# Softmax attention mixed with a Mish layer on one core: a run-time bound on the scores with a second attention behind a branch, a Mish with one reciprocal for four elements, and a later spread of its first layer

## The chip, the cores and the metric

The kernel runs on one core of a Trainium2 chip. A core has five engines that work beside each other, each through its own list of instructions in order: TensorE (PE, matrix products, with its weight loads shown apart as PEld), VectorE (DVE), ScalarE (ACT, functions such as exp), GpSimd (POOL) and SyncE (SP, which issues DMAs). They wait for each other through semaphores. The metric is device time in microseconds (us); the kernel before took 981.92 us in the median of 3 runs (981.38 to 982.19).

## What is computed

```python
S, D, F, H = 2048, 640, 1536, 32          # Dh = 20, bf16 in and out
q, k, v = split(x @ wqkv)                 # x: 2048 x 640
a = softmax(q @ k.T / sqrt(20)) @ v       # 32 heads
a = a @ wo
h = x @ w1 + b1                           # 2048 x 1536
b = (h * tanh(log(1 + exp(h)))) @ w2      # Mish between two layers
g = sigmoid(sum(x * gate_w))              # one value a row
out = g * a + (1 - g) * b
```

The inputs are normal numbers times 0.05 (the Mish layer's weights smaller still).

## The kernel before

**Attention.** Scores are computed transposed: a tile holds 128 keys by 512 queries. One such tile of one head is a unit. The units are ordered in 32 groups of 64: a group is one set of four heads (`p`, 8 of them) and one chunk of 512 queries (`qc`, 4 of them), and runs over 16 blocks of keys (`j`) and the four heads (`t`). A head has only 20 dimensions, so four heads lie on four 32-row strips of PE. The exponentials are taken without subtracting the row maximum. One iteration of the main loop takes 3 units, the next 2, and so on (`WIDTHS`), which makes 819 iterations; a group is 25 or 26 of them. Group 1 begins with iteration 25, group 25 with 640, group 28 with 716, group 30 with 768, group 31 with 793.

In iteration i the list of instructions gets, in this order: the score matmuls of iteration i+1 (`emit_qk`, L616), the exponential of iteration i on ACT from PSUM to a bf16 tile `E` (`emit_exp`, L626), the products of earlier exponentials with V into the accumulator `acc` (`emit_pv`, L656), the steps that are due (`run_later`), and then other PE work (`pump`). V has a column of ones, so that `acc` also gets the sum of each row; at the end of a group `normalise` (L632 to L646) transposes `acc` on DVE, divides, and keeps the result in one of 50 spare tiles, `cells`.

**The other PE work** is cut into chains with a start, a due iteration and a list of pieces, each with a nominal cost in ns: projections to Q and K (`kq_chain`, L255) and V (`v_chain`, L276), the first Mish layer (`h_chain`, L342, 48 tiles of 128 x 512), the second one (`b_chain`, L372, 32 chains of 12 pieces), the output projection (`wo_chain`, L412). `pump` goes through them in order of due iteration. It emits pieces while the work done is behind the summed share that is wanted, up to `BURST` = 700 ns of nominal cost in an iteration, and without that limit when a chain marked hard is about to be late. It also keeps PE at a floor of 0.54 of the iteration's nominal time, with pieces ahead of their share and, where there are none, with matmuls on a tile of ones that nobody reads (`busy_matmul`, L570). Chains accumulate in two PSUM banks (`pp`), which DVE empties.

**Mish** of one tile takes exp(h) on ACT (L305) and then works on DVE on n = e(e+2) and h n/(n+2): two operations at once (L308, L311), a reciprocal in four quarters, one an iteration (L317), and two operations at the end (L320, L324). The result stays in a `cells` tile until all `b_chain`s of its chunk of rows are done. At most two tiles are in the making. The `h_chain`s of the four chunks follow each other from iteration 35 on, 146.6 iterations each, the last one up to iteration 621; the `b_chain`s of a chunk follow 146.6 iterations behind.

**The end.** After the last exponential come the last products with V, `normalise`, eight matmuls (L760), four operations on DVE (L768) that put together the last 512 rows, and four stores (L776), two issued by SP and two by ACT. L804 is the end of the program: waits for all landings, drains, and a barrier over all engines.

Of the kernel before, what the change touches and what calls it, by code (L numbers as in the profile page):

```python
# [14 lines left out]
PSUM = bass.MemoryType.PSUM  # L15


class Chain:
# [11 lines left out]
    def share(self, i):  # L30
        if i >= self.due:
            return self.cost
        if i <= self.start:
            return 0.0
        return self.cost * (i - self.start) / (self.due - self.start)


@with_exitstack
def kernel(
# [25 lines left out]
    inv_sqrt_dh = float(DH) ** -0.5  # L65
    WIDTHS = (3, 2)
    N_CAP = 1.0e30
    NCELL = 50
# [16 lines left out]
    tp = ctx.enter_context(tc.tile_pool(name="tp", bufs=2))  # L85
# [17 lines left out]
    busy = consts.tile([P, QC], BF16, tag="busy")  # L103
    acc = accpool.tile([P, QC], F32, tag="acc")
# [72 lines left out]
    ]  # L177
    iters = []
# [11 lines left out]
    def it_at(G, j=0):  # L190
        k = G * 64 + 4 * j
        return it_of[k] if k < len(units) else NI
# [18 lines left out]
    now = [0]  # L211

# [17 lines left out]
    def transpose_chain(c, u, start, due):  # L230
        def piece():
            ps = pp.tile([P, KT * P], BF16, tag="pp", name="ps")
            transpose_tile(c, u, ps, nc.vector)
            x_ready[c] += 1
# [11 lines left out]
    def kq_chain(wpad, chunk, get_dst, start, due, before=None, copy=None):  # L246
# [16 lines left out]
        def finish():  # L263
            (copy or nc.vector.tensor_copy)(out=get_dst(), in_=box["ps"][:, :])  # L264
# [3 lines left out]
    def v_chain(sts, w, c0, n, h0, start, due, gate=False):  # L268
# [16 lines left out]
        def finish():  # L285
            nh = n // DH
            for i, st in enumerate(sts):
                nc.vector.tensor_copy(
# [13 lines left out]
    def mish_steps(ft, c, h):  # L302
        e = mp.tile([P, QC], F32, tag="e", name="e")
        r = mp.tile([P, QC], F32, tag="r", name="r")
        nc.scalar.activation(e[:, :], h[:, :], ACT.Exp)  # L305

        def first_ops():
            nc.vector.scalar_tensor_tensor(  # L308
                out=e, in0=e, scalar=2.0, in1=e, op0=ALU.add, op1=ALU.mult
            )  # L310
            nc.vector.tensor_scalar(  # L311
                out=r, in0=e, scalar1=N_CAP, scalar2=2.0, op0=ALU.min, op1=ALU.add
            )

        def rec(k):
            a, b = k * P, (k + 1) * P
            nc.vector.reciprocal(out=r[:, a:b], in_=r[:, a:b])  # L317

        def last_ops():
            nc.vector.scalar_tensor_tensor(  # L320
                out=r, in0=e, scalar=N_CAP, in1=r, op0=ALU.min, op1=ALU.mult
            )
            t = taken.pop((ft, c))
            nc.vector.tensor_tensor(out=t, in0=h, in1=r, op=ALU.mult)  # L324
# [3 lines left out]
        at(now[0] + 1, first_ops)  # L328
        for k in range(4):
            at(now[0] + 2 + k, (lambda k=k: rec(k)))  # L330
        at(now[0] + 6, last_ops)

    def h_chain(ft, c, start, due):
# [16 lines left out]
        def finish():  # L350
            h = mp.tile([P, QC], F32, tag="h", name="h")
            nc.vector.tensor_scalar(  # L352
# [11 lines left out]
    def b_chain(s, half, start, due):  # L364
# [15 lines left out]
        def finish():  # L380
            if c not in Bt:
                Bt[c] = stage.tile([P, NU, D], BF16, tag="stage", name="Bt")
            nc.vector.tensor_scalar(  # L383
# [7 lines left out]
            if b_done[c] == 2 * NU:  # L391
                cells.extend(act[(ft, c)] for ft in range(FT))
# [9 lines left out]
    def wo_chain(s, half, start, due, ps_list, base=None, dst=None):  # L402
# [17 lines left out]
        def finish():  # L420
# [5 lines left out]
            else:  # L426
                o = dst()[:, cols]
            nc.vector.scalar_tensor_tensor(  # L428
# [21 lines left out]
    def pads(p):  # L450
# [9 lines left out]
        return fn  # L460

# [45 lines left out]
    span = (m1 - m0) / (NQC + 1)  # L507
    for c in range(NQC):
# [3 lines left out]
        for k, (x, y) in enumerate(spread(a + span + 8, a + 2 * span + 8, 2 * NU)):  # L512
# [8 lines left out]
    for k, (x, y) in enumerate(spread(it_at(G7[last_qc]) + 6, NI - 2, 2 * NU)):  # L521
# [8 lines left out]
        chains.append(wo_chain(s, k % 2, x, y, list(range(NQ - 1)), dst=get_R))  # L530
    chains.sort(key=lambda ch: (ch.due, ch.start))
# [91 lines left out]
    def emit_exp(i):  # L623
# [3 lines left out]
            E[:, 0 : n * QC], S_of.pop(i)[:, 0 : n * QC], ACT.Exp, scale=inv_sqrt_dh  # L627
# [4 lines left out]
    def normalise(G, p, qc):  # L632
        T1 = tp.tile([P, NS, 32], F32, tag="T1", name="T1")
# [15 lines left out]
    pv_hold = [-1]  # L649

    def emit_pv(limit):
        while pv_next[0] + 4 <= limit and pv_hold[0] < now[0]:
# [156 lines left out]
```

## Time and profile before

The profiled execution took 983.07 us; its span, from the first instruction's start to the last one's end, is 981.0 us. The 2.07 us between them lie outside the program. The profiled execution is 1.15 us over the median of the runs.

| part of the span | us |
|---|---|
| up to the first exponential of the attention | 0 to 11.2 |
| the exponentials of the 819 iterations on ACT | 11.2 to 971.1 |
| last products, normalise, last rows, issue of the stores | 971.1 to 978.4 |
| landing of the last stores, waits, drains, barrier | 978.4 to 981.0 |

| engine | busy us | share of the span |
|---|---|---|
| ACT | 959.3 | 98% |
| PE | 841.8 | 86% |
| DVE | 493.2 | 50% |
| POOL | 19.9 | 2% |

A busy time is the union of an engine's instructions. Matmuls are pipelined, so PE's busy share says little about its room. Records of neighbouring instructions on one engine can overlap; then the mean of one is longer than what one more would cost. A row of a group reads: line, engine, operation, written<-read, shapes, count, then busy us and mean ns of one, then the engine's idle time before them and what ended it.

### The profile page before, as it was taken

The numbers are of one execution on the slowest core, as the hardware profiler recorded it, in microseconds if no ns is written. First come the engines' busy times: TensorE is split into PE (matmuls) and PEld (weight loads), VectorE is DVE, ScalarE is ACT, GpSimd is POOL, SyncE is SP. The second block draws the span as 40 slices with busy tenths as digits, with TensorE's granted clock in tenths as the row PEclk, the third lists the DMA queues.
The fourth block names the chain that finished last, engine by engine and source line by source line (L and its number), as shares of the span: only waits on it lengthen the run. The fifth ranks groups of instructions, "written<-read, shape, count | busy, mean of one in ns | idle before, by whom it ended". The sixth has DMA issues, their size and how long they took to land.

```text
span 981.0 us, 14426 instructions
## 1 busy us (share of the span) xinstructions
PE 841.8 (86%) x5834; PEld 309.9 (32%) x5914; DVE 493.2 (50%) x785; ACT 959.3 (98%) x873; POOL 19.9 (2%) x33
## 2 busy tenths in 40 slices
PE   8888888888888888888888888888888888888896
PEld 4333322223333332333222232322323333333332
DVE  4337565566567556655665655565554112112223
ACT  6999999999999999999999999999999999999995
POOL 5000000000000000000000000000000000000000
PEclk9999999999999999999999999999999999999998
DMA  9000010000100010000102001000000000000000
GB/s 272 16 1 21 1 29 1 22 20 2 29 1 21 1 29 1 21 21 1 29 1 54 1 21 29 1 21 1 1 1 1 1 1 14 8 14 15 14 15 34
DMA packets 23515, 19.28 MB, mean 20 GB/s; under 512 B 10025, under 2 KB 22201, under 8 KB 23449
## 3 DMA queue, kind: packets, MB, share of 16 engines
q1 hardware_dynamic: 20696, 11.66, 4.6%
q0 software_dynamic: 1520, 5.94, 2.0%
q8 instruction: 46, 0.75, 0.3%
q10 hardware_dynamic: 1232, 0.76, 0.3%
q14 instruction: 21, 0.16, 0.1%
HBM read 15.73 MB, written 2.62 MB: 19 GB/s over the span
## 4 chain that ended last, share of the span: by engine, by line
ACT 56%; issue 32%; PE 11%; DVE 1%; ACTq 0%
ACT E L626 54%; PE Sp L616 4%; ACT e L305 2%; PE acc L656 2%; PE ps L255 1%; PE ps L412 1%; PE ps L570 1%; PE ps L276 1%; PE acc L679 0%; PE ps L220 0%; DVE ot L768 0%; PE ps L342 0%; DVE xT L228 0%; PE ps L683 0%; PE sa L220 0%
## 5 line engine op out<-in xcount | busy, mean ns | idle before, releaser
L626 ACT ACTIVATE E<-Sp 128x1536 bf16<-128x1536 f32 (+1 forms) x819 | 938.5, 1278 | 4.5 <-PE acc L656 2.5
L616 PE MATMUL Sp<-qT,kT 32*128 32x512 bf16 x2048 | 320.7, 381 | 122.2 <-ACT E L626 103.7
L616 PEld LDWEIGHTS <-kT 32*128 32x128 bf16 x2048 | 128.0, 91 | 345.0 <-issue 310.1
L656 PE MATMUL acc<-E,VA 128*21 128x512 bf16 x2048 | 203.4, 386 | 0.2
L317 DVE RECIPROCAL r<-r 128x128 f32<-128x128 f32 x192 | 166.6, 915 | 1.3
L570 PE MATMUL ps<-busy 128*128 128x512 bf16 (+1 forms) x273 | 88.9, 383 | 1.7 <-DVE ot L428 0.3
L656 PEld LDWEIGHTS <-VA 128*21 128x21 bf16 x2048 | 50.4, 89 | 116.5 <-issue 116.5
L352 DVE TENSOR_SCALAR h<-ps,b1f 128x512 f32<-128x512 f32 x48 | 35.8, 746 | 93.5 <-PE ps L342 88.3
L372 PE MATMUL ps<-w_sb,cell 128*128 128x320 bf16 x384 | 81.3, 304 | 0.0
L308 DVE SCALAR_TENSOR_TENSOR e<-e 128x512 f32<-128x512 f32 x48 | 33.2, 692 | 87.9 <-ACT e L305 87.9
L342 PE MATMUL ps<-xT,w1t 128*128 128x512 bf16 x206 | 67.7, 385 | 2.3 <-issue 2.2
L634 DVE STREAM_TRANSPOSE T<-acc 128x512 f32<-128x512 f32 x32 | 22.9, 717 | 72.1 <-PE acc L656 72.0
L428 DVE SCALAR_TENSOR_TENSOR ot<-ps,g_t,Bt 128x320 bf16<-128x320 f32 x24 | 13.1, 547 | 75.4 <-PE ps L412 75.4
L412 PE MATMUL ps<-wo_sb,cell 128*128 128x320 bf16 x248 | 49.8, 303 | 0.0
L255 PE MATMUL ps<-xT,wqp 128*128 128x512 bf16 x137 | 45.6, 385 | 0.6 <-issue 0.5
L255 PE MATMUL ps<-xT,wkp 128*128 128x512 bf16 x135 | 43.6, 384 | 2.8 <-issue 1.6
L372 PEld LDWEIGHTS <-cell 128*128 128x128 bf16 x384 | 30.1, 97 | 41.0 <-issue 35.6
L383 DVE TENSOR_SCALAR Bt<-ps,g_t 128x320 bf16<-128x320 f32 x32 | 17.3, 540 | 45.5 <-PE ps L372 45.5
L276 PE MATMUL ps<-wv,xT 128*128 128x80 bf16 (+2 forms) x240 | 34.8, 259 | 0.8 <-issue 0.3
L264 DVE CAST qT<-ps 128x512 bf16<-128x512 f32 x31 | 21.1, 682 | 26.9 <-PE ps L255 23.8
L324 DVE TENSOR_TENSOR cell<-h,r 128x512 bf16<-128x512 f32 x48 | 33.4, 696 | 1.6
L320 DVE SCALAR_TENSOR_TENSOR r<-e,r 128x512 f32<-128x512 f32 x48 | 33.0, 687 | 1.1
(66 smaller groups left out, 309.2 us busy)
## 6 DMA issues: line engine op xcount, KB each, us to landing
w1t<-in_B_w_dram SPq DMA_DIRECT2D x14, 480.0 KB, 3.9
out_dram<-ot SPq DMA_DIRECT2D x14, 160.0 KB, 1.8
xs<-in_A_x_dram POOLq DMA_DIRECT2D x3, 640.0 KB, 7.9
w_sb<-in_B_w_dram POOLq DMA_DIRECT2D x1, 1920.0 KB, 12.7
ws<-in_A_wqkv_dram SPq DMA_DIRECT2D x13, 100.0 KB, 3.9
w1t<-in_B_w_dram POOLq DMA_DIRECT2D x2, 480.0 KB, 9.0
wo_sb<-in_A_wo_dram SPq DMA_DIRECT2D x4, 200.0 KB
wv<-in_A_wqkv_dram POOLq DMA_DIRECT2D x1, 400.0 KB, 9.7
```

The source lines that it names most:

```text
L255: nc.tensor.matmul(box["ps"][:, :], lhsT=wpad[:, kt, :, :].rearrange("p h d -> p (h d)"), rhs=xT[:, kt, chunk * QC : (chunk + 1) * QC], st ...
L276: nc.tensor.matmul(box["ps"][:, i, :], lhsT=xT[:, kt, sts[i] * P : (sts[i] + 1) * P], rhs=w[:, kt, c0 : c0 + width], start=(kt == 0), stop ...
L317: nc.vector.reciprocal(out=r[:, a:b], in_=r[:, a:b])
L324: nc.vector.tensor_tensor(out=t, in0=h, in1=r, op=ALU.mult)
L342: nc.tensor.matmul(box["ps"][:, :], lhsT=w1t[4 * c + ft // 3][:, kt, (ft % 3) * P : (ft % 3 + 1) * P], rhs=xT[:, kt, c * QC : (c + 1) * QC ...
L352: nc.vector.tensor_scalar(out=h, in0=box["ps"][:, :], scalar1=b1f[:, ft : ft + 1], scalar2=None, op0=ALU.add)
L372: nc.tensor.matmul(box["ps"][:, :], lhsT=act[(ft, c)][:, u * P : (u + 1) * P], rhs=w2_sb[:, ft, half * HALF : (half + 1) * HALF], start=(f ...
L412: nc.tensor.matmul(box["ps"][:, :], lhsT=OT[(p, c)][:, u * P : (u + 1) * P], rhs=wo_sb[0][:, p, cols], start=(k == 0), stop=(k == len(ps_l ...
L570: nc.tensor.matmul(ps[:, 0:n], lhsT=busy[:, 0:P], rhs=busy[:, 0:n], start=True, stop=True)
L616: nc.tensor.matmul(ps[:, k * QC : (k + 1) * QC], lhsT=kT[p][32 * t : 32 * t + 32, j * P : (j + 1) * P], rhs=qT[G][32 * t : 32 * t + 32, :] ...
L626: nc.scalar.activation(E[:, 0 : n * QC], S_of.pop(i)[:, 0 : n * QC], ACT.Exp, scale=inv_sqrt_dh)
L656: nc.tensor.matmul(acc[32 * t : 32 * t + DH + 1, :], lhsT=VA[:, j, 4 * p + t, :], rhs=E_of.pop(a + t), start=(j == 0), stop=(j == NS - 1), ...
```

## The change

It has four parts.

1. **A bound on the scores, computed beside the attention.** Chains of a new kind (`gram_chain`) multiply blocks of 128 rows of x, and blocks of columns of the Q, K and V weights, with themselves; the largest entry of such a block is the largest squared length. There are 4 chains of 20 matmuls for x, 8 chains of 10 for the Q and K weights, one of 20 and one of 10 for the V weights, each of 128 columns or less, and each read by one to two `tensor_reduce` of DVE from PSUM. `bound_chain` (iterations 691 to 716) adds four matmuls and ten small DVE operations, and leaves 1 or 0 in `safe`.
2. **A branch at the end of the program.** All engines load `safe` into a register; where it is 0, a whole second attention (`attention_with_maximum`, with loops over 32 heads, 16 blocks of queries and 16 blocks of rows, that subtracts row maxima) runs and writes the output again. For it, the four chunks of the Mish half are stored to DRAM (`b_dram`, 640 KB each, issued by SP).
3. **Mish with one reciprocal for four elements.** The four quarters of the denominator are multiplied together pairwise, one quarter's width of reciprocals is taken, and the four results are got back by products. The steps go into a queue of their own (`steps`, `run_slow`): a step is emitted only while less than 900 ns of DVE work is reckoned to be queued.
4. **Spread.** The `h_chain`s get 170.25 iterations for a chunk in place of 146.6, so the last ends at iteration 716 (group 28); the last chunk's `b_chain`s get the 52 iterations after that (724 to 776). `cells` has 48 tiles in place of 50, and `tp` one buffer in place of two.

The core of the diff:

```diff
-    NCELL = 50
+    NCELL = 48
-    tp = ctx.enter_context(tc.tile_pool(name="tp", bufs=2))
+    tp = ctx.enter_context(tc.tile_pool(name="tp", bufs=1))
...
+    def run_slow(i, all_of_it=False):
+        stepped = set()
+        while all_of_it or queued[0] < QUEUE:
+            todo = [x for x in slow if (x[2] <= i and x[1] not in stepped) or all_of_it]
+            if not todo:
+                break
+            x = min(todo, key=lambda x: x[:2])
+            ns, fn = x[3].popleft()
+            vec(ns)
+            fn()
...
-        for k in range(4):
-            at(now[0] + 2 + k, (lambda k=k: rec(k)))
-        at(now[0] + 6, last_ops)
+        def products():
+            V.scalar_tensor_tensor(
+                out=e.rearrange("p (a b) -> p a b", a=2),
+                in0=e.rearrange("p (a b) -> p a b", a=2),
+                scalar=N_CAP, in1=d[:, ::-1, :], op0=ALU.min, op1=ALU.mult,
+            )
+            V.tensor_tensor(out=r[:, 2 * P :], in0=r[:, 0 : 2 * P], in1=r[:, 2 * P :], op=ALU.mult)
+            V.tensor_tensor(out=r[:, Q], in0=r[:, 2 * P : 3 * P], in1=r[:, 3 * P :], op=ALU.mult)
+        def invert():
+            V.reciprocal(out=r[:, Q], in_=r[:, Q])
+        def of_two():
+            V.tensor_tensor(
+                out=r[:, P : 3 * P].rearrange("p (a b) -> p a b", a=2),
...
+            V.tensor_tensor(
+                out=e.rearrange("p (a b) -> p a b", a=2),
...
+        def last():
+            t = taken.pop((ft, c))
+            V.tensor_tensor(out=t, in0=h, in1=e, op=ALU.mult)
+        steps(
+            now[0] + 1,
+            [(1150, n_and_d), (1400, products), (920, invert), (1110, of_two), (690, last)],
+            8,
+        )
...
             if b_done[c] == 2 * NU:
+                nc.sync.dma_start(
+                    out=b_dram[c * QC : (c + 1) * QC, :].rearrange("(u p) d -> p u d", p=P),
+                    in_=Bt[c][:, :, :],
+                )
...
+    def gram_chain(blocks, reads, start, due):
+        box = {}
+        def piece(k):
+            i, kt = divmod(k, KT)
+            if k == 0:
+                box["ps"] = pp.tile([P, 4, P], F32, tag="pp", name="ps")
+            fn, n = blocks[i]
+            nc.tensor.matmul(
+                box["ps"][0:n, i, 0:n], lhsT=fn(kt), rhs=fn(kt),
+                start=(kt == 0), stop=(kt == KT - 1), skip_group_check=True,
+            )
+        def finish():
+            for out, fn in reads:
+                src = fn(box["ps"])
+                vec(150 + src.free_size())
+                nc.vector.tensor_reduce(out=out, in_=src, op=ALU.max, axis=X_AXIS)
+        return Chain(start, due, mm_pieces(KT * len(blocks), piece, 60), finish)
...
-    span = (m1 - m0) / (NQC + 1)
+    last_b = 2 * (it_at(2) - it_at(1))
+    span = (m1 - m0 - last_b) / NQC
...
+        b = a + span + 8
+        for k, (x, y) in enumerate(spread(b, b + (span if c < NQC - 1 else last_b), 2 * NU)):
...
+    ok = nc.values_load(
+        safe[0:1, 0:1], min_val=0, max_val=1,
+        skip_runtime_bounds_check_because="written by comparisons as 0 or 1",
+    )
+    with tc.If(ok == 0):
+        attention_with_maximum(
+            tc, A_wqkv, b_dram, out2d, xT, VA, wo_sb[0], g_t, ident,
+            dict(s=spool, acc=accpool, pp=pp, k=ktp, q=qtp, w=wsp, e=ep, stage=stage, t=tp, m=mp),
+        )
```

In `bound_chain` the branch is passed over (`safe` = 1) where the largest squared row length of x, squared, times the largest squared column lengths of the Q and K weights is at most 40 x 40 / 20 = 80, and that of the V weights times that of x is at most a million. `emit_pv` is written anew with the same order of instructions.

## The prediction

> **What bounds the kernel now.** I read the page's busy times first, then the groups, the waits, the stretches of 100 us, and last the end of the program.
>
> ```profile
> PE 841.8 (86%) x5834; PEld 309.9 (32%) x5914; DVE 493.2 (50%) x785; ACT 959.3 (98%) x873; POOL 19.9 (2%) x33
> ...
> ACT 56%; issue 32%; PE 11%; DVE 1%; ACTq 0%
> ```
>
> ACT is busy for 98% of the span. The chain that ended last gives 32% to "issue" as well, but those are joints between neighbouring ACT instructions, whose records overlap, not another engine's work.
>
> ```profile
> L626 ACT ACTIVATE E<-Sp 128x1536 bf16<-128x1536 f32 x410 | 609.8, 1487 | 4.2 <-PE acc L656 2.5 <-PE Sp L616 1.6
> L626 ACT ACTIVATE E<-Sp 128x1024 bf16<-128x1024 f32 x409 | 437.3, 1069 | 0.3 <-PE Sp L616 0.2
> L305 ACT ACTIVATE e<-h 128x512 f32<-128x512 f32 x48 | 32.3, 672 | 0.0
> ```
>
> These three groups add up to 1079.4 us, more than the span: records of one instruction begin before the last one's end. So I took from the trace's ACT records the distance from end to end. Its median is 1.343 us for a wide exponential, 0.916 for a narrow one and 0.508 for one of Mish. 410 x 1.343 + 409 x 0.916 + 48 x 0.508 = 550.6 + 374.6 + 24.4 = 949.7 us. The stretch is 971.06 - 11.21 = 959.85 us, so all of ACT's lost time together is 10.2 us: 4.3 in eight delays before 35 us, where the first group's projections press, 1.2 in six delays after it (five from 763 us on), and 4.7 in 88 wide exponentials that come 47 ns late, spread evenly over the span. **This 10.2 us is all that a faster PE or DVE can win here.**
>
> ```profile
> PE Sp L616 <- ACT E L626: 103.7, 354, 0.9
> ...
> ACT E L626 <- PE acc L656: 2.5, 3, 1.2
> ...
> ACT E L626 <- PE Sp L616: 1.8, 5, 0.6
> ```
>
> PE waits 103.7 us for ACT, ACT 4.3 us for PE. No row has ACT waiting for DVE. DVE's load lies in the first 700 us:
>
> ```profile
> 500.00:600.00 100.00, 86.00 (x572) 29.83 (x582) 61.45 (x95) 100.00 (x94) 1.73 (x2) 1.00 0.08 19
> ...
> 800.00:900.00 100.00, 88.56 (x639) 34.73 (x643) 18.49 (x34) 100.00 (x89) 0.00 (x0) 1.00 0.03 11
> ```
>
> The third busy figure is DVE: 61.45 us of 100 where Mish runs, 18.49 late. The granted clock (1.00) leaves nothing to win.
>
> **Mish on DVE.** Removed per tile: four reciprocals of 915 ns and two products of 687 and 696; with the first two operations (692 + 433) that is 6.17 us.
>
> ```profile
> L317 DVE RECIPROCAL r<-r 128x128 f32<-128x128 f32 x192 | 166.6, 915 | 1.3
> ```
>
> After: the same first two (1.13 us), a product of 512 (0.69), one of 256 and one of 128, one reciprocal (0.92), one of 256, one of 512 (0.70) and the last (0.70). Rows for 320 (L638, 491 ns) and 512 (L324, 696) give 1.07 ns an element, so 256 costs 0.42 and 128 0.29. Sum 5.27 us, 0.9 less; for 48 tiles DVE saves 43 us. The bound's reads add, by the casts from PSUM (512: 0.68, 256: 0.42 us): 4 x 0.68 + 8 x 0.42 + 1.1 + some 2 for the ten small ones = 9 us. DVE goes from 493 to about 459 us. **On the time: nothing**, since ACT hides all of DVE already. If that cover were gone (ACT waiting for h), the step limit of 900 ns and a normalise of 2.2 us (L634 to L646) could keep an h back by some 3 us against the three iterations (3 x 1.13 us) it is given; I take 0, with 0 to 0.3 for rare delays.
>
> **The Gram blocks on PE.** 80 + 80 + 30 + 4 = 194 matmuls of up to 128 columns. The transposes of the same size go five in 0.44 us (L220 near 7.6 us), 88 ns each: 17 us. They are booked at 60 ns, 11.6 us, and so push aside about 55 of the 273 filler matmuls (213 nominal). The unbooked rest, 5.4 us, lies in 15 chains over 690 iterations, beside PE's 103.7 us of waiting. One chain (weights of set 1, due in iteration 22) falls near 35 us, where ACT does wait for PE: 10 x 88 = 0.9 us of PE, of which up to half may show. Part on the path: 0 to 0.5, taken 0.2 us. The four `b_dram` stores are 640 KB each on SP's queue, against 480 KB for a load that lands in 3.9 us; the DMA share there is a few per cent. They wait for rows that DVE has just written; behind them stand w1 loads that are two tiles early. 0.
>
> **The late spread.** The planner now has, between iteration 706 and 817, three Mish tiles (1.08 us each), 32 - 24 = 8 chains of the second layer (13.4), two chunks of wo (18.0), the rest R (7.8) and four q projections (4.3): 46.7 us nominal in 111 iterations, 421 ns each. Before, the second layer had 146.6 iterations for those 13.4 us; the same stages then asked about 314. ACT's iteration is (1.343 + 0.916)/2 = 1.13 us; a score slot takes 0.33 and a product slot 0.33 x 0.625, which leaves 0.59 us. So 421 fits on average, and the extra first replaces filler (51 in 700 to 800 us). Cells: at iteration 691 there are 27 results of attention and 12 tiles of chunk 2, so only 9 of chunk 3's 12 fit into 48; the last three wait until chunk 2's `b_chain`s end (their last one may not start before 702.7). That makes a knot: some 5 us nominal caught up at 700 ns an iteration, over the 590 that fit. The trace shows its price: near 953 to 958 us five L412 pieces in each of four iterations (0.85 us a burst) cost ACT 0.16 + 0.08 + 0.50 = 0.75 us.
>
> ```profile
> 956.65 0.85 PE L412 MATMUL ps<-wo_sb,cell 128*128 128x320 bf16 x5
> ...
> 958.24 3.74 ACT L626 ACTIVATE E<-Sp 128x1536 bf16<-128x1536 f32 x3 [0.40 <-PE acc L656]
> ```
>
> I take one more such knot, 0.75, with -0.9 (late delays of today gone) to 3 (four knots) as bounds. Fewer cells and one `tp` buffer add no other wait: T1 is used by DVE alone, in order.
>
> **The branch.** No row shows a register load or a branch, so bounds. Today ACT issues the last store at 978.36; it lands, SP passes its waits near 980, and the barrier follows:
>
> ```profile
> L804 SPq EVENT_SEMAPHORE  x11: 17/28/28, 977.6 to 980.9; - x11
> ...
> L804 SPq DRAIN  x3: 7/7/7, 980.2 to 980.5; - x3
> ```
>
> First drain 980.16, last semaphore 980.98 in the trace: 0.82 us for two rounds over the engines; SP's semaphore steps are 0.06 us apart. The second attention writes the output and reads `b_dram`, so an entry that is safe on either path must order itself behind those stores. Lower end: load and branch fit into the 1.5 us in which ACT and SP wait for the landing, 0. Middle: a wait on every engine behind the landing (five steps, 0.3), the jump, semaphores put right on the path not taken (some ten steps, 0.6): with half of another pair of rounds (0.4) and 0.3 for the jump, 1.6 us. Upper end: a pair of rounds on entry and one on exit (1.64), 0.6 of semaphores, and code that has to be brought: like a store's landing, 1.8; in all 4.0. I take 1.6, nearest to the barrier's rows.
>
> The instruction queue's row (46 packets, 0.75 MB, 16.3 KB each; 0.3% of 16 engines' 981 us is 47 us, 1.0 us a packet) shows that code arrives in blocks. [...]
>
> **Sum.** 0.0 (Mish) + 0.2 (Gram) + 0.75 (knot) + 1.6 (branch) = 2.55, say 2.5 us. On the profiled execution's span: 981.0 + 2.5 = 983.5, with 2.07 outside it 985.6. That execution was 1.15 over the median, so against the median: 981.92 + 2.5 = **984.4 us**. What a measurement of this kernel can tell from no change is about 0.2%, 1.96 us: below 979.96 is faster, above 983.88 slower. My forecast stands just over that bound.
>
> **The rivals.**
>
> *All hidden (0.36).* Load and branch run in the landing's shadow or cost one semaphore round (0 to 0.8 us), and PE's 103.7 us take the rest (-0.5 to 1). For it: ACT never waits for DVE, hardly for PE. Against: the second attention's writes must stand behind the last stores. 981.92 + 0.4 = 982.3 us, within 980 to 983.9.
>
> *Faster, the late exponentials (0.06).* One mechanism: the 88 wide exponentials that are 47 ns late come from DVE's traffic beside ACT; with 43 us less of it and even spacing they go, 4.1 us, and the late delays, 0.9. It decides if the branch costs under 3 us. 981.92 - 5.0 + 1.6 = 978.5 us. Against it: they come as often (6 in 22) at 800 to 900 us, with DVE at 18%, as before.
>
> *Late work past the last exponential (0.13).* The knot grows: if chunk 3's tiles end after iteration 750, up to half of its second layer (6.7 us) stands in PE's list ahead of the last products; or code must be fetched on several engines one after another. 981.92 + 1.6 + 0.2 + 4 to 8 = 986 to 992, say 988 us.
>
> *The branch is taken.* x has squared lengths near 640 x 0.0025 = 1.6, the weights' columns too; with 2.2 for the largest each, 2.2 to the fourth is 23, under 80. If it were, 512 passes with 1.343 + 0.916 us of exponentials alone add 1157 us. Under 0.01, left out of the range.
>
> **How the numbers follow.** The forecast, slower by 2.0 to 4.5 us, has 0.45. With the third rival, slower has 0.58; same 0.36; faster 0.06. The range runs from 980.8 (most of the hidden case) to 986.9 (the branch's upper end and one knot: 981.92 + 0.2 + 0.75 + 4.0), leaving out the faster case, the hidden case's low end and most of the late one.
>
> **What would show it.** Right: ACT's exponentials end between 971.5 and 973 us; L305 to the last product at 5.3 us of DVE a tile, DVE busy 455 to 465 us; filler below 230; from the last store's issue to the span's end 4 us in place of 2.6. Wrong: that end still 2.6 us long (hidden), ACT's stretch under 957 us (faster), L372 still running after 940 us, or ACT waiting for h.

## The result and the profile after

The changed kernel takes **986.24 us** in the median of 14 runs (985.31 to 993.48), the kernel before beside it 982.20 (981.38 to 986.11, 14 runs). The medians lie 4.0 us apart; the ratio of the runs is 1.0052, with a 95% interval of 1.0032 to 1.0072. The forecast was 984.4 in a range of 980.8 to 986.9: the sign is right and the time is inside, but the loss is well above the 2.5 us forecast. The upper runs are those in which PE was granted a lower clock (992.5 to 993.5 us at 0.985 or 0.986), so the text also gives medians **at full clock**, of the runs with a mean clock of 0.997 or more: 985.78 (7 runs) against 981.9 to 982.3 for before (the medians in the four groups of runs below), a loss of about 3.6 us (3.5 to 3.9).

The profiled execution took 985.94 us, its span is 984.1, with 1.84 outside (before: 983.07, 981.0, 2.07). Lines of the page after:

```profile
PE 850.7 (86%) x6036; PEld 313.3 (32%) x6115; DVE 467.6 (48%) x859; ACT 960.3 (98%) x873; POOL 19.1 (2%) x33
...
ACT 55%; issue 31%; PE 12%; DVE 1%; ACTq 0%
...
L856 PE MATMUL ps<-busy 128*128 128x512 bf16 x278 | 90.5, 383 | 1.7 <-DVE VA L434 0.4
...
L472 DVE RECIPROCAL r<-r 128x128 f32<-128x128 f32 x48 | 45.5, 948 | 1.2
```

The reciprocals went from 166.6 us to 45.5 and DVE from 493.2 to 467.6, and nothing follows from it: ACT bounds as before. The filler (L856, before L570) was to go under 230 of 273 and is 278. The waits after, in us, times, longest:

```profile
PE Sp L902 <- ACT E L912: 96.8, 313, 1.1
...
ACT E L912 <- PE acc L941: 3.1, 5, 1.2
...
ACT E L912 <- PE Sp L902: 2.5, 9, 0.6
```

There is still no row of ACT waiting for DVE. PE's waits for ACT shrank by 7 us; ACT's for PE grew from 4.3 to 5.6. In stretches (PE, PEld, DVE, ACT, POOL, clock, DMA, GB/s):

```profile
500.00:600.00 100.00, 85.54 (x582) 30.30 (x591) 52.31 (x93) 100.00 (x93) 0.99 (x2) 1.00 0.09 21
800.00:900.00 100.00, 91.65 (x662) 34.25 (x665) 41.26 (x81) 98.72 (x89) 0.00 (x0) 1.00 0.05 18
```

DVE went from 61 to 52 in the middle and from 18 to 41 behind 800 us. There PE went from 88.56 to 91.65, and ACT, which had all of the 100 us, lost 1.28. That is the late spread. Worked out of the ACT records as in the prediction:

| part (us) | before | after | difference |
|---|---|---|---|
| first exponential begins | 11.21 | 10.39 | -0.82 |
| delays of ACT before 36 us | 4.32 | 4.32 | 0 |
| late delays of ACT (over 60 ns, behind 36 us) | 1.17 | 3.85 | **+2.68** |
| many small ones (the 47-ns kind) | 4.51 | 4.68 | +0.17 |
| stretch of the exponentials | 959.85 | 962.72 | +2.87 |
| last exponential to issue of last store | 7.30 | 7.03 | -0.27 |
| that issue to the end of the span | 2.62 | 3.95 | **+1.33** |

The first part is no gain: in the variants below it lies anywhere from 10.35 to 11.99. Nor is the -0.27: PE's clock halves at the end of both programs, in before at 973.03 us, 1.96 behind the last exponential, in the changed kernel at 978.17, 5.06 behind it. So the eight matmuls of the last rows took 472 ns in the median in before (L760) and 299 in the changed kernel (L1058). Two places remain, the late delays and the end.

**The late delays.** Some of them lie where the prediction put its knot. The last three Mish tiles of chunk 3 get h only when the second layer of chunk 2 ends at 843 us:

```profile
L520 DVE TENSOR_SCALAR h<-ps,b1f x3: 745/750/752, 844.9 to 859.6; 128x512 f32<-128x512 f32 x3
```

What PE does then (timeline; L585 is the output projection, L540 the second and L509 the first Mish layer):

```profile
840.29 0.85 PE L540 MATMUL ps<-w_sb,cell 128*128 128x320 bf16 x5
840.47 2.36 ACT L912 ACTIVATE E<-Sp 128x1536 bf16<-128x1536 f32 x2 [0.19 <-PE Sp L902]
841.08 0.39 PE L902 MATMUL Sp<-qT,kT 32*128 32x512 bf16 x2
841.40 0.40 PE L941 MATMUL acc<-E,VA 128*21 128x512 bf16 x4
841.72 0.85 PE L540 MATMUL ps<-w_sb,cell 128*128 128x320 bf16 x5
...
843.16 1.04 PE L509 MATMUL ps<-xT,w1t 128*128 128x512 bf16 x3
...
844.91 3.28 ACT L912 ACTIVATE E<-Sp 128x1024 bf16<-128x1024 f32 x3 [0.45 <-PE ps L509]
```

Between two sets of scores PE does five pieces, 0.85 us, then three large ones, 1.04; the bracket at the right says that the exponential waited. That cost 1.15 us at 840 to 845; 0.78 us of delays followed at 877 to 882, where the second layer of chunk 3 catches up in bursts of the same kind. The rest is 0.33 and 0.46 at 698 and 755 us, the pile at 953 to 960, which before had too (0.75, now 0.89), and some of little more than 60 ns.

**The end.** Issue and landing of the four last stores, before and then after:

```profile
L776 ACTq DMA_DIRECT2D out_dram<-ot x2: 351/352/353, 976.3 to 978.0; - x2
...
DMA to landing us min/median/max: 1.8/1.8/1.8
```

```profile
L1074 SPq DMA_DIRECT2D out_dram<-ot x2: 332/332/332, 977.3 to 978.9; - x2
L1074 ACTq DMA_DIRECT2D out_dram<-ot x2: 350/356/362, 978.1 to 979.8; - x2
...
DMA to landing us min/median/max: 3.3/3.6/3.8
```

The two last of them land 3.8 us (SP's) and 3.3 (ACT's) after their issue. The barrier (L1111, before L804) keeps its form; it only begins later, first drain of SP at 983.2 instead of 980.2:

```profile
L1111 SPq DRAIN  x3: 7/7/7, 983.2 to 983.5; - x3
```

### The profile page after: what moved, and what is told of

Same layout as the page of the kernel before. It is cut to its first block, busy times and chain, and to the rows that moved or that the text cites. A ratio compares the mean times of both kernels' runs of the same rounds, so it can differ in the third digit from the quotient of the medians.

```text
span 984.1 us, 14937 instructions
## 1 busy us (share of the span) xinstructions
PE 850.7 (86%) x6036; PEld 313.3 (32%) x6115; DVE 467.6 (48%) x859; ACT 960.3 (98%) x873; POOL 19.1 (2%) x33
## 4 chain that ended last, share of the span: by engine, by line
ACT 55%; issue 31%; PE 12%; DVE 1%; ACTq 0%
ACT E L912 52%; PE Sp L902 4%; ACT e L451 3%; PE acc L941 2%; PE ps L856 1%; PE ps L399 1%; PE ps L540 1%; PE ps L585 1%; PE ps L509 0%; PE acc L974 0%; PE ps L421 0%; PE ps L363 0%; DVE ot L1066 0%; PE ps L651 0%; DVE xT L371 0%
## 5 line engine op out<-in xcount | busy, mean ns | idle before, releaser
L902 PEld LDWEIGHTS <-kT 32*128 32x128 bf16 x2048 | 122.9, 91 | 340.5 <-issue 311.1
L856 PE MATMUL ps<-busy 128*128 128x512 bf16 x278 | 90.5, 383 | 1.7 <-DVE VA L434 0.4
L540 PE MATMUL ps<-w_sb,cell 128*128 128x320 bf16 x384 | 78.9, 303 | 0.0
L509 PE MATMUL ps<-xT,w1t 128*128 128x512 bf16 x208 | 70.3, 385 | 2.3 <-issue 2.1
L585 PE MATMUL ps<-wo_sb,cell 128*128 128x320 bf16 x248 | 48.9, 302 | 0.0
L399 PE MATMUL ps<-xT,wkp 128*128 128x512 bf16 x138 | 45.2, 384 | 2.3 <-issue 1.1
L472 DVE RECIPROCAL r<-r 128x128 f32<-128x128 f32 x48 | 45.5, 948 | 1.2
L399 PE MATMUL ps<-xT,wqp 128*128 128x512 bf16 x135 | 44.5, 384 | 1.4 <-issue 1.3
L540 PEld LDWEIGHTS <-cell 128*128 128x128 bf16 x384 | 29.4, 97 | 37.6 <-issue 31.6
L409 DVE CAST kT<-ps 128x512 bf16<-128x512 f32 x31 | 21.0, 679 | 32.5 <-PE ps L399 30.4
L490 DVE TENSOR_TENSOR cell<-h,e 128x512 bf16<-128x512 f32 x48 | 33.7, 702 | 1.2
```

What stands on the lines that cost most here:

```text
L399: nc.tensor.matmul(box["ps"][:, :], lhsT=wpad[:, kt, :, :].rearrange("p h d -> p (h d)"), rhs=xT[:, kt, chunk * QC : (chunk + 1) * QC], st ...
L409: nc.vector.tensor_copy(out=get_dst(), in_=box["ps"][:, :])
L472: V.reciprocal(out=r[:, Q], in_=r[:, Q])
L509: nc.tensor.matmul(box["ps"][:, :], lhsT=w1t[4 * c + ft // 3][:, kt, (ft % 3) * P : (ft % 3 + 1) * P], rhs=xT[:, kt, c * QC : (c + 1) * QC ...
L540: nc.tensor.matmul(box["ps"][:, :], lhsT=act[(ft, c)][:, u * P : (u + 1) * P], rhs=w2_sb[:, ft, half * HALF : (half + 1) * HALF], start=(f ...
L585: nc.tensor.matmul(box["ps"][:, :], lhsT=OT[(p, c)][:, u * P : (u + 1) * P], rhs=wo_sb[0][:, p, cols], start=(k == 0), stop=(k == len(ps_l ...
```

## The experiments

Theory at the start: the branch costs about 1.3 us at the end, the late spread 2.7 us of ACT's delays, Mish and Gram nothing. Rivals: the Gram work, the new Mish or the fewer cells cost by themselves. Times are medians (lowest to highest, number of runs), ratios against before on the same chip with 95% intervals. The kernel before beside them had 983.1 (981.41 to 985.4, 35 runs), 983.05 (981.66 to 988.2, 29), 983.13 (981.53 to 988.47, 35) and 982.73 (981.87 to 985.77, 29) in the four groups, 981.9 to 982.3 at full clock.

### Which part costs: four kernels with parts taken out

**Without the branch** (the register load, the branch and the second attention are left out):

```diff
-    ok = nc.values_load(safe[0:1, 0:1], ...)
-    with tc.If(ok == 0):
-        attention_with_maximum(...)
```

> The changed kernel without the register load, the branch and the second attention; the bound is still computed and not used. Theory (the +4.0 us are a pile-up of late work on TensorE, worth 2.7 us of ScalarE delays after 35 us, and the branch, worth about 1.3 us from the last store's issue to the end): about 1.3 us less than the changed kernel, 984.9 us; last store's issue to the end of the span 2.6 us in place of 3.9; ScalarE delays of over 60 ns after 35 us still about 3.9 us in sum. Rival A (the branch is hidden, everything comes from the loop): 986.2, the end part unchanged. Rival B (the Gram work is the cause): 986 less the branch, the same as the theory here.

986.75 us (984.04 to 992.70, 12), ratio 1.0044 [1.0024, 1.0064]. Half of the runs had a clock of 0.991 or less; at full clock 984.59, that is 1.2 under the changed kernel. The end part is 2.35 us.

**The spread of before, with the branch:**

```diff
-    span = (m1 - m0 - last_b) / NQC
+    span = (m1 - m0) / (NQC + 1)
-        ... spread(b, b + (span if c < NQC - 1 else last_b), 2 * NU)
+        ... spread(b, b + span, 2 * NU)
```

> The changed kernel with the old spread of the two Mish layers (146.6 iterations for each chunk, the last chunk's second layer over 146.6 too), still 48 cells. Theory: the pile-up at 835 to 905 us goes, delays after 35 us fall from 3.9 to about 1.2 us, 983.5 us. Rival A (Gram work shifts the planner and delays ScalarE): delays stay at 3 us or more, 985.7. Rival B (a lower granted TensorE clock is the cause, not the schedule): the median follows the clock of the runs, with several runs at 988 to 993 as before.

985.40 us (983.57 to 988.11, 12), 1.0026 [1.0018, 1.0035]. No run had the full clock; a line through the runs' times over their clocks gives 983.7 there, against 985.9 for the changed kernel by the same means: 2.1 less. Late delays 1.69 us, end part 4.21.

**Both edits:**

> The changed kernel with the old spread and without the branch; Gram blocks, new Mish, 48 cells and the stores to DRAM are in. Theory: both parts add, 982.2 us, the same as before within 0.2%. Rival A (Gram work costs 1 to 2 us): 983.5 or more. Rival of the Mish (43 us less on VectorE shows after all): under 981.

984.16 us (982.17 to 988.62, 12), 1.0016 [1.0005, 1.0027]; at full clock 982.21 (2 runs), the time of before. So the new Mish, 48 cells and all of the Gram work, with their stores, cost nothing that shows in the time at full clock. Over all runs the loss is 0.5 to 2.7 us; ten of the twelve had a clock of 0.985 to 0.995. The profile shows one delay that comes of the Gram work, 0.41 us at 272 us: the Gram block (L651) reads the weights `wkp`, POOL may write the next set over them only then, and the K projections (L399) and with them the scores come late. All four kernels with the old spread and the Gram work have it, none with the late spread.

```profile
271.17 0.52 POOL L275 COPY wkp<-ws 128x400 bf16<-128x400 bf16 x1 [0.66 <-PE ps L651]
...
271.75 0.39 PE L399 MATMUL ps<-xT,wkp 128*128 128x512 bf16 x1 [0.70 <-POOL wkp L275]
...
272.57 3.71 ACT L911 ACTIVATE E<-Sp 128x1536 bf16<-128x1536 f32 x3 [0.30 <-PE Sp L901]
```

**Without branch, Gram blocks, bound and stores of the Mish half** (the new Mish and the late spread stay; the bound isn't computed):

> The changed kernel without Gram blocks, bound, stores to DRAM and branch: new Mish, new spread and 48 cells alone. Theory: the pile-up is the spread's own, delays after 35 us about 3 us or more, 984.7 us, as without the branch alone. Rival A (the pile-up needs the Gram work): delays about 1.2 us, 982.2.

985.73 us (984.93 to 995.72, 12), 1.0046 [1.0022, 1.0070]; at full clock 984.94, against 984.59 with the Gram work. Late delays 3.78 us. The Gram work is not the cause. The waits of ACT behind 690 us separate the two spreads; first before, then the old spread with all the rest, then the changed kernel:

```profile
ACT E L626 <- PE acc L656: 0.4, 1, 0.4
```

```profile
ACT E L911 <- PE acc L940: 0.4, 1, 0.4
ACT E L911 <- PE Sp L901: 0.2, 1, 0.2
```

```profile
ACT E L912 <- PE acc L941: 1.0, 3, 0.4
ACT E L912 <- PE Sp L902: 0.8, 4, 0.2
ACT E L912 <- PE ps L509: 0.5, 1, 0.5
ACT E L912 <- PE ps L856: 0.2, 1, 0.2
```

0.4, 0.6 and 2.5 us: the waits come with the late spread.

### Why the spread costs: cells, bursts, or the place itself

**56 cells in the changed kernel:**

```diff
-    NCELL = 48
+    NCELL = 56
```

> The changed kernel with 56 spare tiles in place of 48, all else as changed. Theory (the pile-up starts because the last three Mish tiles of chunk 3 find no free tile until chunk 2's second layer has ended at 843 us): 27 results + 24 tiles fit, the three tiles are made on time, chunk 3's second layer starts at iteration 724 and not 738, ScalarE delays after 35 us fall from 3.9 to about 1.5 us, 983.8 us where the clock is not disturbed (985.8 now). Rival (52 iterations for that layer are too few by themselves): delays stay above 3 us, 985.5.

991.54 us (987.68 to 1004.11, 7), 1.0055 [1.0039, 1.0071]; the ratio leaves out the three runs above 1003 us. This was a miss. PE was at half clock for long stretches, so the run tells nothing of cells (stretches of its profile, columns as above):

```profile
836.00:843.00 7.00, 4.13 (x27) 1.43 (x28) 4.79 (x12) 6.52 (x7) 0.00 (x0) 1.00 0.00 0
843.00:887.00 44.00, 43.23 (x195) 9.98 (x198) 14.57 (x30) 31.98 (x27) 0.00 (x0) 0.50 0.07 23
```

For 44 us the granted clock is 0.50, PE is full (43.23), and ACT gets 32 of the 44. Ahead of it PE was idle for 41% of 7 us; its longest wait there, 1.78 us (2.28 for its weight load), is that of the bound's matmuls for four small DVE operations.

**Those four operations eight iterations earlier, with 56 cells:**

```diff
+        def tops():
+            ...
+        at(start - 8, tops)
```

> The changed kernel with 56 cells, where VectorE's four operations ahead of the bound's four matmuls are issued eight iterations earlier, so that TensorE doesn't wait for them (2.3 us with 56 cells before). Theory (that wait left a 3.41 us stretch so empty that the clock halved at 843 us and stayed so for 44 us): no such stretch, no wait of these matmuls for VectorE, undisturbed time about 984, slowest run under 994. Rival (the clock falls there for another reason): again runs of 995 to 1004.

985.44 us (983.57 to 994.23, 12), 1.0037 [1.0015, 1.0060]. The wait and the 44 us are gone (PE is busy 5.56 us of 836 to 843), but four of the runs have a clock of 0.991 or less by a dip, a stretch at half clock, elsewhere (6.8 us at 149.7 in the profile). It doesn't beat before. But the knot is gone here too: besides the delays of that dip the late ones are 1.68 us instead of 3.85, with none at 840 to 845 and 877 to 882. A line through the runs' times over their clocks gives 984.05 at full clock, 1.8 under the changed kernel by the same means.

**56 cells without Gram, bound and branch** (as the fourth kernel, so no bound is computed):

> New Mish and new spread with 56 cells, without Gram blocks, bound, stores to DRAM and branch, so that no wait of the bound's matmuls is in the way. Theory (missing cells make the knot): ScalarE delays after 35 us about 1.5 us in place of 3.8, last Mish tile done before 860 us in place of 872, 983.2 us at an undisturbed clock in place of 984.9. Rival (52 iterations are too few by themselves): delays 3 us or more, 984.5.

983.98 us (983.25 to 985.12, 12), 1.0008 [0.9996, 1.0020]; no clock under 0.995. It is 0.96 under its twin with 48 cells at full clock. Late delays are 1.87 us, besides 0.89 at a dip of 3.41 us at 832.7. The last Mish tile is done at 852 us instead of 872, and the place of the knot looks like this:

```profile
840.62 0.39 PE L509 MATMUL ps<-xT,w1t 128*128 128x512 bf16 x1
...
841.58 0.61 PE L509 MATMUL ps<-xT,w1t 128*128 128x512 bf16 x2
...
842.82 0.30 PE L581 MATMUL ps<-wo_sb,cell 128*128 128x320 bf16 x1
```

One to two pieces between scores instead of three to five; the delays at 840 to 845 and 877 to 882 are gone.

**The late spread alone, in the kernel before** (old Mish, 50 cells):

> The kernel before with the new spread alone: old Mish, 50 cells, no Gram blocks, no branch. Theory (the spread carries the loop's loss by itself): delays after 35 us 2.5 to 3.5 us in place of 1.2, 1.5 to 2.2 us slower than before. Rival (the loss needs the new Mish's queue of steps or the Gram work beside it): within 0.4 us of before.

983.82 us (983.46 to 984.37, 11), 1.0008 [0.9999, 1.0016]. All clocks are 0.996 or more; against the full-clock runs of before it loses 1.9 us (984.02 to 982.08). Late delays 2.42 us instead of 1.17, at 699 and 756 us above all.

**The same with 48 cells and one `tp` buffer:**

> The new spread with the old Mish, 48 cells and one T1 buffer, no Gram blocks, no branch: against the same with 50 cells (2.4 us of delays, 984.0 us, no run with a clock under 0.996). Theory (cells): delays 3.5 us or more, 985 us, and some runs with a granted clock of 0.986 or less. Rival (the new Mish's steps cause the second part of the delays and the low clocks): 984.0 us and clocks of 0.996 and more.

988.96 us (986.87 to 999.46, 12), 1.0073 [1.0048, 1.0099]. The delays at 841 to 845 (1.14 us) are back, as is the last tile at 872 us, with the old Mish. **So the knot comes of the two cells less under the late spread, not of the new Mish** (nor of the one `tp` buffer, which the kernel with 56 cells has too). All of its runs also had a clock below 0.997, one as low as 0.975; a line through them gives 986.0 at full clock, 2.0 over the 50 cells.

**Smaller bursts in the changed kernel:**

```diff
-    BURST = 700.0
+    BURST = 500.0
```

> The changed kernel with BURST 500 in place of 700: an iteration ends its extra pieces after four of 140 ns nominal, not five. Theory (five pieces of 0.16 us beside a score slot of 0.33 and product slots of 0.2 overrun an iteration of 1.13 us, four nearly fit): delays after 35 us about 1.5 us, 984 us at an undisturbed clock. Rival (the sum of late work is too much for the stretch): delays as before or work left past the last exponential, 986 or more.

985.02 us (983.38 to 994.57, 12), 1.0030 [1.0012, 1.0049]. Early delays 4.31 to 3.06 us, of which 0.53 come back at 40 us, just behind the limit of that sum; those of 840 to 845 from 1.15 to 0.64, of 877 to 882 from 0.78 to 0.38. In the knot the burst's length is the means by which the work reaches ACT. The delays at 698 and 755 us stay as they were, 0.33 and 0.46: this limit on the bursts does not set them.

**Smaller bursts with the old spread, branch kept:**

> The changed kernel, branch included, with the old spread and BURST 500. Theory: delays after 35 us, 1.7 with the old spread alone, fall to 0.5 to 1; 983.1 us at an undisturbed clock, 0.6 less than the old spread alone and 2.7 less than the change. Rival (bursts are not what delays ScalarE): same as the old spread alone, 983.7.

983.30 us (982.42 to 988.57, 11), 1.0001 [0.9985, 1.0018]. With bound and branch this is the time of before.

**Smaller bursts in the kernel before:**

> The kernel before with BURST 500 in place of 700, nothing else. Theory (bursts of five pieces delay ScalarE in the kernel before as well): the delays before 35 us fall from 4.3 to about 3.6 with what is newly late near 40 us, those at 950 to 960 us from 0.8 to 0.2; 1.2 to 1.6 us faster than before, about 980.8 at an undisturbed clock. Rival (the gain with the old spread came from elsewhere): within 0.3 us of before.

981.74 us (980.21 to 987.08, 12), 0.9993 [0.9974, 1.0012]. At full clock 980.86 against 981.91, but four of the runs fell to 0.987 to 0.989; no gain is shown.

### What the branch costs

**The branch kept, its body one memset** (the second attention is left out):

```diff
     with tc.If(ok == 0):
-        attention_with_maximum(...)
+        nc.vector.memset(vn, 0.0)
```

> The changed kernel with the register load and the branch, but one memset in place of the second attention behind it (which these inputs pass over in either kernel). Theory (the load, the compare and the semaphores end before the last stores land; the cost is the code that the jump over the second attention has fetched by the same DMA engines, which holds the stores' last packets back): no code packet in the last 5 us, the last two stores land 1.8 us after their issue in place of 3.3 to 4.4, end part 2.4 to 2.8 us in place of 3.9 to 4.6, 984.6 us at an undisturbed clock. Rival (load, compare and semaphores themselves): end part 3.9, 985.8.

984.67 us (983.94 to 992.49, 10), 1.0025 [1.0009, 1.0041]; at full clock 984.40, 1.4 under the changed kernel and no slower than without any branch (984.59). So the load, the compare and the jump cost nothing that shows in these times; what stands behind the branch does. In the changed kernel's trace, the loads (L1079) and branches (L1083) of the engines:

```profile
L1079 SPq TENSOR_LOAD <-safe x1: 507/507/507, 979.3 to 979.3; - x1
L1079 ACTq TENSOR_LOAD <-safe x1: 477/477/477, 980.2 to 980.2; - x1
```

```profile
L1083 PEldq COMPARE_BRANCH  x1: 451/451/451, 978.7 to 978.7; - x1
...
L1083 SPq COMPARE_BRANCH  x1: 45/45/45, 979.9 to 979.9; - x1
...
L1083 ACTq COMPARE_BRANCH  x1: 54/54/54, 980.7 to 980.7; - x1
```

ACT, the last one, takes up again at 981.2 us, long before the last landing at 983.1 that the barrier waits for. What delays the landing shows in the DMA queues. The last 8 us of the changed kernel (queue, packets, MB, share of 16 engines; then KB of an issue and us to landing), and the last 8 us with the small body:

```profile
q8 instruction: 1, 0.02, 1.2%
q14 instruction: 3, 0.02, 1.1%
...
out_dram<-ot SPq DMA_DIRECT2D x2, 160.0 KB, 3.8
out_dram<-ot ACTq DMA_DIRECT2D x2, 160.0 KB, 3.3
```

```profile
q10 hardware_dynamic: 288, 0.33, 11.6%
q1 hardware_dynamic: 288, 0.33, 11.6%
issues: line engine op xcount, KB each, median us to landing
out_dram<-ot SPq DMA_DIRECT2D x2, 160.0 KB, 1.8
out_dram<-ot ACTq DMA_DIRECT2D x2, 160.0 KB, 1.8
```

Four packets of code run between 979.9 and 982.2 us. None runs in the last 8 us of the kernel before, of the one without the branch or of the one with the small body, where these stores land 1.8 us after their issue. The packets of the stores show how they act. Each store is 128 packets of 1280 bytes. In the changed kernel 120 of the last one of SP start by 980.3 us; the other eight, a sixteenth, start from 981.48 on, as the 16 KB packet of code ends (979.93 to 981.50), and eight of ACT's follow them from 982.28 on. That would fit one of the page's 16 DMA engines held by code, an inference from the sixteenth. In before all 128 packets of the last store start within 0.55 us (978.86 to 979.41).

### The clock, and a kernel with all of it mended

**Filler during the Gram chains** (`pump` breaks off where the current chain isn't due and has no bank to put filler into; Gram chains had none; the conjecture: PE's thin place near 150 us, where the kernel without branch has a dip at 149.36, lets the clock fall):

```diff
+        def bank():
+            ...
-        return Chain(start, due, mm_pieces(KT * len(blocks), piece, 60), finish)
+        return Chain(start, due, mm_pieces(KT * len(blocks), piece, 60), finish, bank=bank)
```

> The changed kernel where a Gram chain lends its PSUM bank to the filler matmuls, as the other chains do, so that the floor holds while such a chain waits for its share. [...]

986.17 us (984.93 to 993.33, 12), 1.0027 [1.0016, 1.0038]; at full clock 985.71, no change. Near 150 us the profile has no dip, but neither has that of the changed kernel; PE is busy for 2.99 of 3.80 us there instead of 2.75. A dip of 20.5 us came at 853.8, in the lull behind the knot. So the place got fuller, and the low clocks did not go: two runs of twelve have 0.986.

**Old spread, 56 cells, bursts of 500, the bound's reads ahead and filler in the Gram chains; bound, branch and second attention kept:**

> The changed kernel with bound, branch and second attention kept, and the repairs together: old spread, 56 cells, BURST 500, the bound's reads eight iterations ahead, filler in Gram chains. Theory: loop delays after 35 us 0.5 to 1.5 us, the branch's 1.2 us stay; 982.4 us at an undisturbed clock, within 0.1% of before in the median, and fewer low clocks than with the old spread and small bursts alone. Rival (the parts get in each other's way): 983.5 or more.

983.39 us (981.55 to 986.16, 12), 1.0007 [0.9994, 1.0021]. The one run at full clock is 981.55. The low clocks were to become rarer and did not: five runs had 0.991. It and the old spread with small bursts are the best kernels found with the bound, level with before within their intervals; none beats it for sure.

## Why the prediction was half right

| term of the sum | predicted | measured | by |
|---|---|---|---|
| Mish | 0 | 0 | both edits undone: 982.2 at full clock |
| Gram blocks | 0.2 | 0 (0.4 with the old spread) | with and without: 984.59 and 984.94; the delay at 272 us |
| late spread, one knot | 0.75 | 2.1 to 2.4 | spread undone with and without branch |
| branch | 1.6 | 1.1 to 1.4 | branch or its body taken out |

**Mish: right.** One tile takes 5.29 us of DVE (predicted 5.27), there is no wait for h, and the 47-ns delays stay (87 of them in before by a narrow count, 91 after) with DVE at 52 instead of 61: the rival that put them on DVE's traffic is out. DVE's total was 8 us off, 467.6 for 459. The records added up fall from 515.4 to 482.6 us, about as worked out; but the busy time is their union, and the overlaps fell too, from 22.2 to 15.0. Sums of records must not be taken off a union.

**Gram: right in size, wrong in the filler and in the place.** What shows of it is not PE's time but the hold on `wkp`, and not near 35 us. The blocks pushed no filler aside in total (273 to 278): from 700 to 800 us it fell from 51 to 36, but the spread asks less of PE earlier (second layer 10.1 us instead of 13.0 from 600 to 700).

**The step that failed** is the late spread: "I take one more such knot, 0.75, with -0.9 ... to 3 (four knots) as bounds." The mechanism was there, tile for tile: exactly three tiles waited for cells until chunk 2's second layer ended. But the term is too small: undoing the spread wins 2.1 to 2.4 us, not 0.75. Two things are wrong in it. First, the one knot was priced by the pile at 953 to 958 us, 0.75; with its echo at 877 to 882 it made six delays of 1.93 us. Second, the sum had nothing for other places, and 0.33 and 0.46 us came at 698 and 755 with 48, 50 and 56 cells alike (0.59 instead of 0.46 without Gram). At 755 four K projections in a row stand between two sets of scores in the kernel with the spread alone:

```profile
753.88 1.24 PE L255 MATMUL ps<-xT,wkp 128*128 128x512 bf16 x4
...
755.86 3.71 ACT L628 ACTIVATE E<-Sp 128x1536 bf16<-128x1536 f32 x3 [0.49 <-PE acc L658]
```

At 698 PE has itself just waited 0.81 us for ACT; why the exponential is late there is open. The prediction weighed the mean (421 of 590 ns an iteration fit) and priced one exception; but the pieces of a knot come in bursts of up to 700 ns, and each of them can pass the room of one iteration while the mean is far below it.

How the loss divides between the knot and the rest is known only roughly. The times give 0.96 (48 against 56 cells without Gram), 1.8 (with everything else in and the bound's reads ahead) and 2.0 (old Mish, 48 against 50) for the knot, and 1.9 to 2.1 for the rest (50 or 56 cells against before). The stretch of the exponentials in the profiles gives 1.8 for the knot and less for the rest: 961.26 us with the spread alone and, without the dip's 0.89, 961.07 with 56 cells, against 959.85 before and 962.90 with 48 cells without Gram. The medians of the times also hold the start: both profiles begin their exponentials at 11.2 us, as that of before does, and the full-clock runs of the spread alone lie in two groups, 983.6 to 983.8 and 984.2 to 984.4, the profiled one in the upper. That the start makes the groups is not shown.

**The branch: right in size, by the wrong cause.** 1.6 was built from waits, a jump and semaphores behind the landing. None of these came: engines load and branch while the stores fly, and the small body shows them free (984.40 us against 984.59 without any branch). The 0.3 us of a jump and 0.6 of semaphores in the sum show in no run as time behind the landing; a compare-and-branch took 0.045 to 0.45 us, ahead of it, and in their place stand 1.5 to 2.0 us of later landing. The term that was real is "code that has to be brought", which the prediction held for the upper end, and it costs not by stopping an engine (ACT and SP take up again within 0.5 us of their branch, before the landing) but by delaying the stores' landing. The 1.0 us a packet of the prediction's instruction row lies near the cost by luck: there were four packets, the one on q8 took 1.57 us, and what they delayed was data.

**Rivals.** All hidden: false by the interval. Late work past the last exponential: false, L540 ends at 921.8 us and the part from the last exponential to the last store is 0.3 us shorter. Branch taken: false, since the program ends at once. Two sums of the prediction are off: the late rival's lower end is 987.7 us by its own terms and not 986, and 88 times 47 ns is 4.1 us and not 4.7, which is what the larger delays leave of the 10.2.

**What was not on the list** is the clock, of which the prediction says only that it "leaves nothing to win". At full clock the changed kernel loses 3.6 us; the rest of its mean loss (the ratio of the runs makes 5.1 us, within 3.1 to 7.1) is from runs with a lower one: 4 of 14 at 0.991 or less, against 4 of the 128 runs of before that stood beside the experiments. Why the changed kernel has more of them is not shown.

## What to carry over

A mean load that fits says little where work is handed out in bursts: compare the longest burst with the room between two instructions of the bounding engine, at each place where a deadline moves. When work is moved later, follow the storage that it holds: here two cells less made three tiles wait, and the wait came back as bursts. A branch that is never taken was paid here by what stands behind it (1.4 us for the second attention against one memset), so keep its body short, or put its decision where no transfer that counts is in flight (the second was not tried). And look at the clock of every run: here it cost 1.5 of 5.1 us, and filling one thin place on PE did not make the low clocks go.

## What the runs showed of the hardware

**Packets of code held packets of data back.** With one packet of code of 16 KB and three of 8 KB beside them, two 160 KB stores landed 1.5 to 2.0 us later than the 1.8 us without: in the changed kernel eight of a store's 128 packets start only as the packet of 16 KB ends.

**PE's granted clock fell to a half for 3.41 us, or for 20.5, 23.9 and 44 us,** without PE being idle for long (1.78 us at most in the 7 us ahead of the 44, 1.19 us in all in the 7.5 ahead of the 20.5, 1.14 in the 3.2 ahead of the 23.9), and a full PE didn't end the long ones at once (23.79 of 23.9 us and 43.23 of 44 busy). In the kernel without branch, one short dip (the third to last column group is the clock), and 23.9 us in the kernel with the small body, with the stretch ahead of it:

```profile
149.40:152.80 3.40, 2.92 (x20) 1.28 (x19) 2.75 (x7) 2.86 (x3) 0.00 (x0) 0.50 0.00 0
```

```profile
146.00:149.20 3.20, 2.06 (x15) 0.67 (x14) 2.22 (x4) 3.20 (x5) 0.00 (x0) 1.00 0.51 117
149.20:173.10 23.90, 23.79 (x104) 5.28 (x101) 6.09 (x12) 18.14 (x16) 0.00 (x0) 0.50 0.00 1
```

A short dip cost ACT about 1 us: in the kernel without branch it is idle for 1.04 of the 10 us from 150 on, and in the one with 56 cells without Gram the dip delayed it by 0.89. A run's time rises by some 6.4 us for each 0.01 that the mean clock is lower, by a line through the 14 runs of the changed kernel. Two of the long dips follow places where PE's work is thin (64% busy here, 59% in the kernel with 56 cells), but the one of 20.5 us follows 7.5 us with PE busy for 84%, and in the changed kernel's own profiled execution the place near 150 us (2.75 us of 3.80, 72%) has full clock.

A step of 3.413 us, the length of the shortest dip, fits the changes of the clock: in the kernel without branch the dips begin at 149.36, 616.98 and 855.92 us, 137.0 and 70.0 steps apart, and the traces have full clock for 965.97 us in before (7.06 to 973.03) and for 972.80 in the changed kernel (5.37 to 978.17), 283.0 and 285.0 steps. Counted in steps, PE is busy for 51% of the one ahead of the halving at the end in before and for 35% in the changed kernel, but there the step before that, with 60%, passed. In the loop the thinnest steps of both (2.31 and 2.23 us of 3.41) passed, and so did stretches of 3.41 us that lie across two steps with 58% (from 202.6 us on in before) and 57% (from 849.5 on in the changed kernel). What exactly the clock goes by stays open. No kernel tried here kept the low clocks away for a known reason: the spread alone with 50 cells has none under 0.996, 56 cells without Gram none under 0.995 though one dip in its profile, and the kernel built to be free of them was not (0.991 in five runs of 12).
